# A chunked-attention and two-MLP kernel: the first blocks' values fetched by fewer loads, memory rows from GpSimd's queue

## The chip, the cores and the metric

The kernel runs on one NeuronCore of a Trainium2 chip. The time is the device time of one execution in microseconds (us). Profiles are of one execution each; the "span" is the time from its first to its last instruction. PE is TensorE, ACT ScalarE, DVE VectorE, POOL GpSimd, and SP is SyncE, which here only issues DMAs.

## The reference, cut to what matters

Attention in chunks of 32 queries: each chunk sees 8 memory rows and a window of its own keys (16 to the left, 8 to the right). Two dense layers follow, over 3072 tokens.

```python
B, H, S, D = 4, 8, 768, 64;  n_mem = 8;  chunk, left_ctx, right_ctx = (32, 16, 8)
for c in range(S // chunk):
    l_start, r_end = max(0, c_start - left_ctx), min(S, c_end + right_ctx)
    k_full = concat([mem_k, k[:, :, l_start:r_end]], axis=2)
    v_full = concat([mem_v, v[:, :, l_start:r_end]], axis=2)
    a = softmax(scale * q_c @ k_full.T)
    out[:, :, c_start:c_end] = a @ v_full
x = out.transpose(0, 2, 1, 3).reshape(B * S, H * D)          # 3072 x 512
h = x @ w_in;   g = h * clip(h + 3, 0, 6) / 6;  x = g @ w_out     # 512 -> 2048 -> 512
h = x @ w_in2;  g = where(h >= 1, h, where(h <= -1, 0, (h + 1)**2 / 4));  y = g @ w_out
```

## The kernel before, in words

**Work and tiles.** The tokens are cut into 6 tiles of 512. A tile needs the attention of four "superblocks" `s` of 128 queries (four chunks each), 24 in all. A superblock is: `scores` (L460, PE, into `sc`), a maximum over keys (L474, DVE), exponentials (L485, ACT), normalisation (L491 to L495, DVE), a transpose (L504, DVE, into `tr`), `values` (L529 in the first two tiles, PE, into `pv`), and a split of the result into a high and a low part, `xhi` (L575, ACT) and `xlo` (L579, DVE). Then the first layer runs per tile: 16 steps of `hidden` (L603 to L605, 12 matmuls into `ph`) and `project` (L652 to L654, 12 matmuls into `py`), and after six tiles the second layer does the same on `ymid`.

**Loads.** Queries and keys of a block `j` of 96 queries come in one load of 128 partitions (`load_block`, tile `q_sb`, 448 KB). Blocks below `NEARLY` lie in an array `qkv` whose rows also hold the values (512 numbers, 2048 B of a row); later ones lie in `qk` and `vv`, where a value row is cut into two of 1024 B. A superblock's values (`load_values`, tile `v_sb`, 512 KB) are, per chunk, 64 rows: 8 of the memory and 56 of the window. In the first two tiles a chunk's 64 rows stand as two columns on 32 partitions, so `load_values` cuts each chunk into pieces at rows 8, 32 and 64 and joins neighbours that continue each other; a superblock takes 7 to 9 loads of 8, 24, 32, 64 or 96 rows. The 32 weight pieces of the first layer come as 64-bit numbers (`raw`, 512 KB each, L279) and are decoded on ACT and DVE (L286 to L312) into `w`.

**Order.** A planner (`Plan.run`, L136 on) simulates the engines with a cost for every task and writes each engine's instructions in one fixed order; buffers are handed out by it too. A load is a task of SP with a cost of 430 ns, and `kb` of data that take their turn on one shared bandwidth. Every load waits for the one that stands eight places ahead of it on SP's queue, since eight completion semaphores are shared in turn. Where the planner sees PE idle in the first 60 us of its own time, matmuls on a constant tile (`warm`, L765, "fillers" below) are put in.

Of the kernel before, what the change touches and what calls it, by code (L numbers as in the profile page):

```python
# [22 lines left out]
NMEM = 8  # L23
CHUNK, LEFT, RIGHT = 32, 16, 8
# [7 lines left out]
NC = DM // 128  # L32
NF = DFF // 128
GRP = 4
NEARLY = 6
LATE_W = GRP * (QB + KB)
T = 512
NT = NTOK // T
# [38 lines left out]
class Plan:  # L77
# [58 lines left out]
    def run(self, at):  # L136
        free = dict(at)
        bw = 0
        last_kind = None
        ready = {e: [] for e in free}  # L140

        def put(t):
            for e, _ in t.ways:
                ready[e].append(t)

        for t in self.tasks:
            if not t.left:
                put(t)
        left = len(self.tasks)
        order = []  # L150
        while left:
            best = None
            for e, ts in ready.items():
                found = []
                blocked = set()
                for t in sorted(ts, key=lambda t: (t.key, t.n)) if e == "SP" else ts:
                    est = max(free[e], t.ready)
                    taken = [] if blocked & {p for b in t.bufs if not b.slot for p in b.pools} else self.slots_for(t)
                    if taken is None or len(taken) < sum(b.slot is None for b in t.bufs):
                        if e == "SP":  # L160

                            blocked.update(p for b in t.bufs if b.slot is None for p in b.pools)
                        continue
                    found.append((max([est, *(s.at + HOP for s in taken)]), t))
                if not found:
                    continue
                first = min(x[0] for x in found)
                if e == "PE" and last_kind:

                    same = [x for x in found if x[1].kind and x[0] <= free[e] + WINDOW]  # L170
                    found = same or found
                est, t = min(
                    (x for x in found if x[0] <= first + WINDOW), key=lambda x: (x[1].key, x[1].n)
                )
                if best is None or est < best[0]:
                    best = est, e, t
            assert best, ("no task can start", [
                (t.n, t.emit.__qualname__, t.key, [b.name for b in t.bufs if b.slot is None])
                for ts in ready.values() for t in ts][:20])
            est, e, t = best  # L180
            for x, _ in t.ways:
                ready[x].remove(t)
            ns = dict(t.ways)[e]
            if e == "PE":
                ns += CHANGE * (bool(t.kind) != bool(last_kind))
                last_kind = t.kind
            t.eng, t.start = e, est
            free[e] = est + ns
            t.end = est + ns + TAIL[e]
            if t.kb:  # L190
                bw = max(bw, t.end + 1900) + t.kb / 0.39
                t.end = bw
            for b, s in zip([b for b in t.bufs if b.slot is None], self.slots_for(t)):
                b.slot, s.used = s, True
            for b in t.bufs:
                b.users -= 1
                b.free_at = max(b.free_at, t.end)
                if not b.users:
                    b.slot.used, b.slot.at = False, b.free_at
            for d in t.then:  # L200
                d.left -= 1
                d.ready = max(d.ready, est)
                if not d.left:
                    put(d)
            for d in t.next:
                d.left -= 1

                alone = all(x == e for x, _ in d.ways)
                d.ready = max(d.ready, est + ns if alone else t.end + HOP)
                if not d.left:  # L210
                    put(d)
            order.append(t)
            left -= 1
        order.sort(key=lambda t: (t.start, t.n))
        return order
# [11 lines left out]
def fused_kernel(ctx: ExitStack, tc: tile.TileContext, qkv, qk, vv, wpk, const, out):  # L227
# [40 lines left out]
    def weight(l, f, z, key, after=()):  # L268
# [43 lines left out]
            eng.tensor_tensor(out=t[:, 1], in0=words()[2], in1=t[:, 0], op=ALU.subtract)  # L312

        lo, hi = (raw, "lo"), (raw, "hi")
        add(("SP", 430), key - 4, load, writes=[lo, hi], kb=512, after=after)
        add([("DVE", dve(512, True)), ("ACT", 575)], key - 0.5, shift, writes=[lo])
        add(("ACT", 575), key - 0.5, rebase, writes=[hi])
        add(("DVE", dve(512)), key - 0.4, sign, [hi], [lo])
# [21 lines left out]
    def wide(j):  # L340
        return j * NCH >= 2 * T // CHUNK

    def load_block(j, key):

        early = key < 0

        over = key > 1.75 * NF
        far = 3 * (not early)  # L350
        w = KB + KC if wide(j) else KB
        q = q_buf[j] = Buf(
            ["in"] + ["w"] * ((early or over) and not wide(j)), [128, NP * (QB + w)], F32, "q_sb",
            **({"w": 1} if early else {}),
        )
        if j < NEARLY:
            src = qkv[j, :, :WQ]
        else:
            src = qk[2 * (j - NEARLY):2 * (j - NEARLY) + 2].rearrange("g d w -> (g d) w")
        after = last_w if over else ()  # L360
        if not wide(j):
            add(("SP", 430), key - 6 - far, lambda e: nc.sync.dma_start(tile_of(q), src), writes=[(q, 0)], kb=448, after=after, line="load")
            return
        k4 = lambda: tile_of(q)[:, NP * QB:].rearrange("p (a t) -> p a t", a=NP)
        add(
            ("SP", 430), key - 6 - far, lambda e: nc.sync.dma_start(
                k4()[:, :, :KB], src[:, NP * QB:].rearrange("p (a t) -> p a t", a=NP)
            ), writes=[(q, 1)], kb=256, after=after, line="load",
        )
        add(  # L370
            ("SP", 430), key - 6 - far, lambda e: nc.sync.dma_start(tile_of(q)[:, :NP * QB], src[:, :NP * QB]),
            writes=[(q, 0)], kb=192, after=after, line="load",
        )

        def spread(e):
            k = k4()
            cast(e, k[:, :, KB + NMEM:], k[:, :, NMEM + CHUNK:KC + CHUNK])
            cast(
                e, k[:, :, 2 * CHUNK:2 * CHUNK + 2 * KC].rearrange("p a (b t) -> p a b t", b=2)[:, :, :, :NMEM],
                k[:, :, :NMEM].unsqueeze(2).to_broadcast([128, NP, 2, NMEM]),  # L380
            )

        add([("DVE", 330), ("ACT", 400)], key - 4.5, spread, [], [(q, 1)])

    def load_values(s, key):
# [4 lines left out]
        v = v_buf[s] = Buf(  # L390
            ["lv"] + ["w"] * early, [128, 2, H * D], F32, "v_sb", **({"w": 1} if early else {}),
        )
        runs = []
        for c in range(NSB):
            j, i = divmod(s * NSB + c, NCH)
            cuts = [0] + [NMEM] * (i > 0) + [CHUNK] * (not late) + [KC]
            for a, b in zip(cuts, cuts[1:]):
                row = a if b <= NMEM else a + CHUNK * i
                p, col = (64 * (c % 2) + a, c // 2) if late else (CHUNK * c + a % CHUNK, a // CHUNK)
                for r in runs:  # L400
                    if r[0] == j and r[1] + r[4] == row and r[2] + r[4] == p and r[3] == col:
                        r[4] += b - a
                        break
                else:
                    runs.append([j, row, p, col, b - a])
        for n, (j, row, p, col, m) in enumerate(sorted(runs, key=lambda r: (r[3], r[2]))):
            if j < NEARLY:
                src, rows = qkv[j, row:row + m, WQ:], lambda t: t
            else:
                g = 2 * (j - NEARLY)  # L410
                src, rows = vv[g:g + 2, row:row + m, :].rearrange("g k c -> k g c"), lambda t: t.rearrange("k (g c) -> k g c", g=2)
            add(
                ("SP", 430), key - 5 - 3 * (not early),
                lambda e, src=src, rows=rows, p=p, m=m, col=col: nc.sync.dma_start(rows(tile_of(v)[p:p + m, col]), src),
                writes=[(v, n)], kb=2 * m, line="load v",
            )
        v.parts = len(runs)

    def block(s, key):
        first = key < 0  # L420
# [89 lines left out]
        def values(e, m=None):  # L510
# [23 lines left out]

        qs = sorted({j for j, _ in places})
        add(
            ("PE", 750 if all(wide(j) for j in qs) else 1450), key - 4, scores,
            [(q_buf[j], x) for j in qs for x in range(1 + wide(j))],
            [(sc[0], 0), (sc[1], 0)], hold=[st], line="scores", kind="a",
        )  # L540
# [6 lines left out]
            add(("ACT", 1150), key - 3, lambda e, h=h: exps(e, h), [(sc[h], 0), (sm, 2)], [(st, h), (sm, 0, h)])  # L547
        add(("DVE", 280), key - 2.5, weigh, [(sm, 0, 0), (sm, 0, 1)], [(sm, 3)])
        add(("DVE", dve(512)), key - 2.4, norm, [(sm, 3)], [(st, 0), (st, 1)])
        of_v = [(v, n) for n in range(v.parts)]  # L550
        if late:
            for c in chunks:
                for b in range(2):
                    add(("DVE", dve(256)), key - 2.2, lambda e, c=c, b=b: turn_part(e, c, b), [(st, 0), (st, 1)], [(tr, c, b)])
            ts = [(tr, c, b) for c in chunks for b in range(2)]
            add(("PE", 750), key - 1, values, [*ts, *of_v], [(x, 0) for x in pv], line="values", kind="a")
        else:
            add(("DVE", 635), key - 2.2, turn, [(st, 0), (st, 1)], [(tr, 0)])
            for m in range(2):
# [128 lines left out]
    def second_x(n):  # L688
        xhi, xlo = xbuf[NT + n]
        key = NK + NF * n  # L690
        for c in range(NC):
            x = Buf(["in", "o", "st"], [128, T], F32, "x2raw")
            add(
                ("SP", 430), key - 8 + 0.5 * c, lambda e, c=c, x=x: nc.sync.dma_start(tile_of(x), ymid[n, :, c]),
                [("ymid", n, c)], [(x, 0)], kb=256, after=[h_tasks[key - NF]],
            )
            ways = [("ACT", act(T)), ("DVE", dve(T, True))]
# [138 lines left out]
```

## Time and profile before

| | |
|---|---|
| median of 3 runs | 1162.54 us (1161.67 to 1164.28) |
| the profiled execution's own time | 1161.94 us |
| its span | 1160.1 us |
| PE busy in the span | 1144.1 us (99%) |
| DVE, ACT, POOL busy | 614.9, 457.8, 0.2 us |
| granted TensorE clock, mean | 0.986 |

The profiled execution lasted 1.84 us longer than its span. A sum made on the span is brought to a time by adding that; the profiled execution is 0.6 us under the median of the three runs. PE's busy time counts fillers as work, so a busy PE is not a PE that does the reference's work.

### The profile page before, as it was taken

How to read it: one execution, taken by the hardware profiler on the slowest of the kernel's cores; microseconds unless marked ns; L12 is line 12 of the kernel's file. 1: busy time of each engine (PE TensorE's matmuls, PEld its weight loads, DVE VectorE, ACT ScalarE, POOL GpSimd, SP SyncE). 2: the span in 40 equal slices, each digit the busy share in tenths (PEclk: the TensorE clock that was granted, in tenths of full speed). 3: DMA queues.
4: the chain of work that ended last, by engine and by line, in shares of the span. 5: the costliest groups of instructions: out<-in, count | busy, mean ns of one | idle time of the engine just before them, and what ended most of it. 6: DMA issues, size and time to landing. Idle time of an engine off the chain costs nothing.

```text
span 1160.1 us, 20860 instructions
## 1 busy us (share of the span) xinstructions
PE 1144.1 (99%) x8766; PEld 939.5 (81%) x8766; DVE 614.9 (53%) x1116; ACT 457.8 (39%) x1083; POOL 0.2 (0%) x4
## 2 busy tenths in 40 slices
PE   8899999999999999999999999999999999999998
PEld 6687888888887888888888888888888888888887
DVE  2589955445555445643899634434434434433433
ACT  3599633334333333333788423223223223222221
POOL 0000000000000000000000000000000000000000
PEclk8699999999999999999999999999999999999999
DMA  6791131112112112210656300200200200000100
GB/s 207 249 396 55 57 100 35 51 54 90 48 35 87 51 51 74 70 38 19 200 183 216 91 1 1 73 1 1 73 1 1 73 1 1 37 1 1 37 1 37
DMA packets 48644, 81.05 MB, mean 70 GB/s; under 512 B 5158, under 2 KB 28582, under 8 KB 48550
## 3 DMA queue, kind: packets, MB, share of 16 engines
q1 hardware_dynamic: 48550, 79.71, 20.9%
q8 instruction: 69, 1.13, 0.4%
q14 instruction: 25, 0.20, 0.1%
HBM read 67.11 MB, written 12.58 MB: 69 GB/s over the span
## 4 chain that ended last, share of the span: by engine, by line
PE 97%; DMA 1%; issue 1%; ACT 1%; DVE 0%; SPq 0%; DVEq 0%; ACTq 0%
PE ph L603 15%; PE ph L604 15%; PE ph L605 15%; PE py L652 8%; PE po L657 8%; PE po L659 8%; PE po L658 8%; PE py L653 7%; PE py L654 7%; PE sc L460 2%; PE pv L529 2%; PE pv L519 1%; PE pv L765 1%; DMA ymid<-ysb 0%; DMA v_sb<-qkv 0%
## 5 line engine op out<-in xcount | busy, mean ns | idle before, releaser
L603 PE MATMUL ph<-xhi,w 128*128 128x512 f32 x768 | 300.5, 391 | 0.0
L604 PE MATMUL ph<-xlo,w 128*128 128x512 f32 x768 | 299.2, 390 | 0.0
L605 PE MATMUL ph<-xhi,w 128*128 128x512 f32 x768 | 299.0, 389 | 0.0
L626 ACT ACTIVATE r<-r,bias 128x512 f32<-128x512 f32 x96 | 69.3, 722 | 286.6 <-DVE r L623 286.6
L633 DVE TENSOR_TENSOR glo<-r,ghi 128x512 fp32r<-128x512 f32 x192 | 132.6, 690 | 81.9 <-ACT ghi L632 80.4
L632 ACT CAST ghi<-r 128x512 fp32r<-128x512 f32 x192 | 119.5, 623 | 133.7 <-DVE r L629 71.2
L603 PEld LDWEIGHTS ph<-xhi,w 128*128 128x128 f32 x768 | 144.5, 188 | 30.5 <-ACT raw L286 0.3
L605 PEld LDWEIGHTS ph<-xhi,w 128*128 128x128 f32 x768 | 144.3, 188 | 30.2
L604 PEld LDWEIGHTS ph<-xlo,w 128*128 128x128 f32 x768 | 144.5, 188 | 29.7
L652 PE MATMUL py<-ghi,w 128*128 128x512 f32 x384 | 153.5, 400 | 1.3 <-DVE ysb L679 1.3
L654 PE MATMUL py<-ghi,w 128*128 128x512 f32 x384 | 149.8, 390 | 0.0
L653 PE MATMUL py<-glo,w 128*128 128x512 f32 x384 | 149.8, 390 | 0.0
L657 PE MATMUL po<-w,ghi 128*128 128x512 f32 x384 | 149.4, 389 | 0.0
L658 PE MATMUL po<-w,ghi 128*128 128x512 f32 x384 | 149.4, 389 | 0.0
L659 PE MATMUL po<-w,glo 128*128 128x512 f32 x384 | 149.4, 389 | 0.0
L619 DVE SCALAR_TENSOR_TENSOR r<-r,ph 128x512 f32<-128x512 f32 x96 | 65.8, 685 | 154.0 <-ACT r L616 153.3
L623 DVE TENSOR_SCALAR r<-ph 128x512 f32<-128x512 f32 x96 | 66.3, 691 | 152.2 <-PE ph L605 152.2
L616 ACT ACTIVATE r<-ph,bias 128x512 f32<-128x512 f32 x96 | 66.2, 689 | 191.9 <-PE ph L605 191.9
L629 DVE TENSOR_TENSOR r<-ph,r 128x512 f32<-128x512 f32 x96 | 66.3, 690 | 74.7 <-ACT r L626 74.7
L652 PEld LDWEIGHTS py<-ghi,w 128*128 128x128 f32 x384 | 72.0, 188 | 18.4 <-DVE ysb L679 1.7
L654 PEld LDWEIGHTS py<-ghi,w 128*128 128x128 f32 x384 | 72.1, 188 | 15.2
L659 PEld LDWEIGHTS po<-w,glo 128*128 128x128 f32 x384 | 72.1, 188 | 15.0
(52 smaller groups left out, 962.7 us busy)
## 6 DMA issues: line engine op xcount, KB each, us to landing
raw<-wpk SPq DMA_DIRECT2D x64, 512.0 KB
ymid<-ysb SPq DMA_DIRECT2D x24, 256.0 KB
x2raw<-ymid SPq DMA_DIRECT2D x24, 256.0 KB
out<-osb SPq DMA_DIRECT2D x24, 256.0 KB
q_sb<-qk SPq DMA_DIRECT2D x21, 256.0 KB
v_sb<-vv SPq DMA_DIRECT2D x43, 112.0 KB
q_sb<-qk SPq DMA_DIRECT2D x21, 192.0 KB
v_sb<-vv SPq DMA_DIRECT2D x24, 128.0 KB
```

The costliest lines, as they stand in the source:

```text
L603: P.matmul(p, whi[:, c, :], xh[:, c, :], start=(c == 0), stop=False)
L604: P.matmul(p, whi[:, c, :], xl[:, c, :], start=False, stop=False)
L605: P.matmul(p, wlo[:, c, :], xh[:, c, :], start=False, stop=(c == NC - 1))
L626: add(("ACT", act(T) + 100), k + 0.35, lambda e: A.activation(out=rt(), in_=rt(), func=AF.Square, bias=bias[:, 1:2], scale=0.5,), [], [(r, ...
L632: add(("ACT", act(T)), k + 0.5, lambda e: A.copy(tile_of(ghi), rt()), [(r, 0)], [(ghi, 0)])
L633: add(("DVE", dve(T)), k + 0.6, lambda e: V.tensor_tensor(out=tile_of(glo), in0=rt(), in1=tile_of(ghi), op=ALU.subtract,), [(r, 0), (ghi, ...
L652: P.matmul(y, w2hi, gh, start=first, stop=False)
L653: P.matmul(y, w2hi, gl, start=False, stop=False)
L654: P.matmul(y, w2lo, gh, start=False, stop=last)
L657: P.matmul(y, gh[:, t], wt[:, 0], start=first, stop=False)
L658: P.matmul(y, gh[:, t], wt[:, 1], start=False, stop=False)
L659: P.matmul(y, gl[:, t], wt[:, 0], start=False, stop=last)
```

## The change

`load_values` of the first two tiles (superblocks 0 to 7) no longer cuts a chunk at rows 8 and 32. One load on SP's queue takes all chunks of a superblock that lie in the same block `j`: its source pattern has a step of 32 rows between the two columns, so each partition gets rows `r` and `r + 32`. For every chunk but a block's first, this puts 8 window rows where the memory's rows belong; a second load of 8 rows (16 KB), issued from GpSimd's queue, then writes the memory rows over them. It waits for the first load. There are 21 such loads. `NEARLY` becomes 11, so that all blocks of the first two tiles lie in `qkv`. The planner's numbers change too: SP's cost of a load from 430 to 450, 470 or 800 ns, the bandwidth model for loads that are not on SP, and the costs of `scores`, of late `values` and of `turn_part`.

```diff
-NEARLY = 6
+NEARLY = 11
...
             if t.kb:
                 bw = max(bw, t.end + 1900) + t.kb / 0.39
-                t.end = bw
+                t.end = bw if e == "SP" else t.end + 1900 + t.kb / 0.1
...
+        if not late:
+            v.parts = []
+            c = 0
+            while c < NSB:
+                j, i = divmod(s * NSB + c, NCH)
+                n = min(NSB - c, NCH - i)
+                rows = qkv[j, CHUNK * i:CHUNK * (i + n), WQ:]
+                src = bass.AP(rows.tensor, rows.offset, [rows.ap[0], [CHUNK * rows.ap[0][0], 2], rows.ap[1]])
+                part = (v, c)
+                v.parts.append(part)
+                add(
+                    ("SP", 470), key - 5, lambda e, src=src, p=CHUNK * c, n=n: nc.sync.dma_start(
+                        tile_of(v)[p:p + CHUNK * n], src
+                    ), writes=[part], kb=128 * n, line="load v",
+                )
+                for x in range(c + (i == 0), c + n):
+                    v.parts.append((v, "m", x))
+                    add(
+                        ("POOL", 1000), key - 4.5, lambda e, j=j, p=CHUNK * x: nc.gpsimd.dma_start(
+                            tile_of(v)[p:p + NMEM, 0], qkv[j, :NMEM, WQ:]
+                        ), [part], [(v, "m", x)], kb=16, line="load m",
+                    )
+                c += n
+            return
...
-            cuts = [0] + [NMEM] * (i > 0) + [CHUNK] * (not late) + [KC]
+            cuts = [0] + [NMEM] * (i > 0) + [KC]
...
-                ("SP", 430), key - 5 - 3 * (not early),
+                ("SP", 800), key - 8,
...
-            ("PE", 750 if all(wide(j) for j in qs) else 1450), key - 4, scores,
+            ("PE", 800 if all(wide(j) for j in qs) else 1450), key - 4, scores,
...
-                    add(("DVE", dve(256)), key - 2.2, ...
+                    add(("DVE", 450), key - 2.2, ...
-            add(("PE", 750), key - 1, values, ...
+            add(("PE", 1070), key - 1, values, ...
```

On SP, the program begins before the change with two blocks' queries and keys and then the first superblock's values in eight pieces:

```order
L362 DMA q_sb<-qkv 128x896 x2
L414 DMA v_sb<-qkv 32x512
L414 DMA v_sb<-qkv 8x512
L414 DMA v_sb<-qkv 24x512
L414 DMA v_sb<-qkv 8x512
L414 DMA v_sb<-qkv 24x512
L414 DMA v_sb<-qkv 32x512
L414 DMA v_sb<-qkv 96x512
L414 DMA v_sb<-qkv 32x512
L362 DMA q_sb<-qkv 128x896
```

After the change the same queue begins with all of the first tile's loads and goes on to the weights (`raw`), with only single loads of later blocks between them:

```order
L363 DMA q_sb<-qkv 128x896 x2
L407 DMA v_sb<-qkv 96x2x512
L407 DMA v_sb<-qkv 32x2x512
L363 DMA q_sb<-qkv 128x896
L407 DMA v_sb<-qkv 64x2x512 x2
L363 DMA q_sb<-qkv 128x896
L407 DMA v_sb<-qkv 32x2x512
L407 DMA v_sb<-qkv 96x2x512
L363 DMA q_sb<-qkv 128x896 x2
L407 DMA v_sb<-qkv 96x2x512
L407 DMA v_sb<-qkv 32x2x512
L280 DMA raw<-wpk 128x512 x2
```

Behind these rows follow one `q_sb`, six `raw`, one `q_sb`, six `raw`, and then the fifth superblock's values, the first load of values that needs a buffer which an earlier superblock held. The third `q_sb` moved from the eleventh place to the fifth, and the first `raw` from the 39th to the 15th.

GpSimd's queue held no DMA; between its constants and its end it now has the 21 loads of memory rows, 2, 3, 3 and 2 of them for the first four superblocks:

```order
L853 MEMSET const-float32-1.0 128x1
L853 MEMSET const-bfloat16-1.0 128x1
L853 MEMSET const-uint8-127 128x1
L859 UNCONDITIONAL_BRANCH
L414 DMA v_sb<-qkv 8x512 x21
L859 UNCONDITIONAL_BRANCH
```

On PE, before the change, 50 fillers stand behind the second superblock's scores, then the first superblock's values (`pv`), then the third's scores:

```order
L765 LDWEIGHTS warm
L765 MATMUL pv<-warm 128x128
L529 MATMUL pv<-tr,v_sb 64x32 x64
L460 MATMUL sc<-q_sb 32x8 x6
L460 MATMUL sc<-q_sb 32x56 x2
L460 MATMUL sc<-q_sb 32x64 x2
```

After it, the third's scores stand ahead of the first's values, with 9 fillers before and 17 behind them, and the fourth's scores follow the values:

```order
L792 LDWEIGHTS warm
L792 MATMUL pv<-warm 128x128
L556 MATMUL pv<-tr,v_sb 64x32 x64
L487 MATMUL sc<-q_sb 32x8 x4
L487 MATMUL sc<-q_sb 32x64 x2
L487 MATMUL sc<-q_sb 32x56 x4
```

Both programs run the same scores and values ahead of the first `hidden` matmul: scores of superblocks 0 to 4, values of 0 to 3. The fillers ahead of it are 26, 15, 50, 11, 6, 42, 5, 42 and 8 before (205), and 26, 9, 9, 17, 31, 2, 7 and 8 after (109). A filler is two instructions, a weight load and a matmul. Behind the first `hidden` matmuls stand 17 fillers before, and 22 and 2 after. Further on, up to the ninth superblock's scores, PE's rows differ in the places where scores and values stand between the layer's matmuls; behind those the pattern is the same in both.

## Rows read from the trace of the kernel before

**Rows 1.** The page: engines, and the instruction DMA queue (packets, MB, share).

```profile
PE 1144.1 (99%) x8766; PEld 939.5 (81%) x8766; DVE 614.9 (53%) x1116; ACT 457.8 (39%) x1083; POOL 0.2 (0%) x4
...
q8 instruction: 69, 1.13, 0.4%
```

**Rows 2.** Stretches: us; busy (instructions) of PE, PEld, DVE, ACT, POOL; clock, DMA, GB/s.

```profile
0.00:54.40 54.40, 43.57 (x1245) 35.99 (x1246) 21.80 (x63) 22.54 (x97) 0.20 (x4) 0.74 0.69 224
...
61.50:130.00 68.50, 68.47 (x855) 55.29 (x847) 64.58 (x124) 61.27 (x153) 0.00 (x0) 1.00 0.50 185
```

**Rows 3.** What PE waited for in 0:60: total us, times, longest us.

```profile
PE pv L529 <- issue: 4.5, 2, 2.9
PE sc L460 <- issue: 4.1, 4, 1.9
...
PE sc L460 <- DMA q_sb<-qkv: 0.8, 1, 0.8
```

**Rows 4.** Engines by stretch, cut where PE's idle times ended.

```profile
0.00:6.67 6.67, 5.69 (x95) 4.16 (x97) 0.13 (x3) 1.49 (x2) 0.20 (x4) 1.00 0.66 212
6.67:11.19 4.52, 3.39 (x151) 2.72 (x138) 1.07 (x5) 2.47 (x16) 0.00 (x0) 1.00 0.59 170
11.19:19.13 7.94, 6.04 (x255) 5.63 (x254) 4.91 (x14) 3.55 (x21) 0.00 (x0) 0.99 0.49 144
19.13:24.66 5.53, 3.95 (x127) 3.48 (x126) 0.93 (x3) 0.00 (x0) 0.00 (x0) 0.50 0.91 275
24.66:30.50 5.84, 4.43 (x127) 3.47 (x127) 0.97 (x4) 4.45 (x22) 0.00 (x0) 0.50 0.85 291
30.50:39.55 9.05, 8.54 (x254) 7.80 (x255) 5.54 (x15) 3.24 (x21) 0.00 (x0) 0.69 0.66 216
39.55:47.52 7.97, 5.02 (x127) 4.67 (x128) 3.98 (x8) 2.86 (x7) 0.00 (x0) 0.71 0.99 360
47.52:52.23 4.71, 4.34 (x127) 3.27 (x126) 2.09 (x6) 2.32 (x7) 0.00 (x0) 0.50 0.41 125
...
52.23:61.18 8.95, 8.94 (x127) 6.19 (x129) 8.05 (x16) 8.28 (x28) 0.00 (x0) 0.76 0.81 282
```

**Rows 5.** DMA queues in 39.6:45.1, 45.1:45.2, 47.5:49.5, 49.5:49.7, 61.2:65.1, 65.1:65.3: packets, MB, share.

```profile
q1 hardware_dynamic: 526, 1.85, 97.4%
...
q8 instruction: 1, 0.02, 61.4%
...
q1 hardware_dynamic: 278, 0.42, 68.0%
...
q8 instruction: 1, 0.02, 35.0%
...
q1 hardware_dynamic: 447, 1.63, 102.5%
...
q8 instruction: 1, 0.02, 33.6%
```

**Rows 6.** The chain that ended last, 0:56: start us, us, what.

```profile
5.95 3.91 DMA q_sb<-qkv
...
50.90 0.96 PE ph L765 x2
...
52.24 2.74 PE ph L765 x6
54.98 0.43 PE ph L603
```

**Rows 7.** SP's first issues of values in order of time: start us, us.

```profile
1.65 4.13 SPq L414 DMA_DIRECT2D v_sb<-qkv  x8
```

**Rows 8.** Fillers after the first `hidden`, and a stretch with all engines of DMA busy.

```profile
58.39 2.03 PE L765 MATMUL sc<-warm 128*128 128x256 bf16 x17
...
60.35:65.00 4.65, 4.65 (x128) 3.98 (x128) 4.62 (x10) 2.72 (x6) 0.00 (x0) 1.00 1.03 416
```

**Rows 9.** PE's groups in 0:54.42: busy us, mean ns, idle before.

```profile
L529 PE MATMUL pv<-tr,v_sb 32*64 32x32 f32 x512 | 11.9, 255 | 4.5 <-issue 4.5
```

More of the change, by code (lines that the diff above doesn't have):

```diff
@@ L314, in weight @@
         lo, hi = (raw, "lo"), (raw, "hi")
-        add(("SP", 430), key - 4, load, writes=[lo, hi], kb=512, after=after)
+        add(("SP", 450), key - 4, load, writes=[lo, hi], kb=512, after=after)
         add([("DVE", dve(512, True)), ("ACT", 575)], key - 0.5, shift, writes=[lo])
@@ L361, in load_block @@
         if not wide(j):
-            add(("SP", 430), key - 6 - far, lambda e: nc.sync.dma_start(tile_of(q), src), writes=[(q, 0)], kb=448, after=after, line="load")
+            add(("SP", 450), key - 6 - far, lambda e: nc.sync.dma_start(tile_of(q), src), writes=[(q, 0)], kb=448, after=after, line="load")
             return
@@ L365, in load_block @@
         add(
-            ("SP", 430), key - 6 - far, lambda e: nc.sync.dma_start(
+            ("SP", 450), key - 6 - far, lambda e: nc.sync.dma_start(
                 k4()[:, :, :KB], src[:, NP * QB:].rearrange("p (a t) -> p a t", a=NP)
@@ L370, in load_block @@
         add(
-            ("SP", 430), key - 6 - far, lambda e: nc.sync.dma_start(tile_of(q)[:, :NP * QB], src[:, :NP * QB]),
+            ("SP", 450), key - 6 - far, lambda e: nc.sync.dma_start(tile_of(q)[:, :NP * QB], src[:, :NP * QB]),
             writes=[(q, 0)], kb=192, after=after, line="load",
@@ L395, in load_values @@
             j, i = divmod(s * NSB + c, NCH)
-            cuts = [0] + [NMEM] * (i > 0) + [CHUNK] * (not late) + [KC]
+            cuts = [0] + [NMEM] * (i > 0) + [KC]
             for a, b in zip(cuts, cuts[1:]):
                 row = a if b <= NMEM else a + CHUNK * i
-                p, col = (64 * (c % 2) + a, c // 2) if late else (CHUNK * c + a % CHUNK, a // CHUNK)
+                p, col = 64 * (c % 2) + a, c // 2
                 for r in runs:
@@ L416, in load_values @@
             )
-        v.parts = len(runs)
+        v.parts = [(v, n) for n in range(len(runs))]
     def block(s, key):
@@ L549, in block @@
         add(("DVE", dve(512)), key - 2.4, norm, [(sm, 3)], [(st, 0), (st, 1)])
-        of_v = [(v, n) for n in range(v.parts)]
+        of_v = v.parts
         if late:
@@ L553, in block @@
                 for b in range(2):
-                    add(("DVE", dve(256)), key - 2.2, lambda e, c=c, b=b: turn_part(e, c, b), [(st, 0), (st, 1)], [(tr, c, b)])
+                    add(("DVE", 450), key - 2.2, lambda e, c=c, b=b: turn_part(e, c, b), [(st, 0), (st, 1)], [(tr, c, b)])
             ts = [(tr, c, b) for c in chunks for b in range(2)]
-            add(("PE", 750), key - 1, values, [*ts, *of_v], [(x, 0) for x in pv], line="values", kind="a")
+            add(("PE", 1070), key - 1, values, [*ts, *of_v], [(x, 0) for x in pv], line="values", kind="a")
         else:
@@ L693, in second_x @@
             add(
-                ("SP", 430), key - 8 + 0.5 * c, lambda e, c=c, x=x: nc.sync.dma_start(tile_of(x), ymid[n, :, c]),
+                ("SP", 450), key - 8 + 0.5 * c, lambda e, c=c, x=x: nc.sync.dma_start(tile_of(x), ymid[n, :, c]),
                 [("ymid", n, c)], [(x, 0)], kb=256, after=[h_tasks[key - NF]],
```

## The prediction

> **What bounds the kernel now.** The page comes first: PE is busy 99% of the span [rows 1], so time can only be won or lost where PE does something other than the reference's matmuls. The stretches show where that is [rows 2]. From 61.5 to 130 us PE is busy 68.47 of 68.50 us at the full clock, and the pattern goes on to the end. Up to 54.4 us it is busy 43.57 us, at a mean granted clock of 0.74, and 205 of its matmuls there are fillers. Everything this change touches lies in that start. So the question is when the first `hidden` matmul can run (54.98 us in the chain [rows 6]), and what follows moves with it.
>
> The view of waits says what PE stood still for in the start, and the answer is unusual: 4.5 us before `pv` and 4.1 us before `sc` with the releaser "issue" [rows 3], that is, for nothing that a semaphore tells. Cutting the start at the ends of those idle times gives the key table [rows 4]. Between them PE ran 127+126, 127+127, 127+128 and 127+126 matmuls and weight loads, and 255+254 and 254+255 where no stop shows at an edge between: always about 254, or twice that. The first row is cut where this count leads back to, at 95+97 = 192, and the last where it leads on to, 61.18 us (127+129). The page has a DMA queue of instructions with 69 packets and 1.13 MB, 16.4 KB each; 8766+8766 instructions over 69 packets is 254 per packet [rows 1]. So a packet is a block of PE's program, and PE's idle times end at block edges: it waits for its own instructions.
>
> The DMA queues show how late a block comes [rows 5]. PE enters a block at 39.55 us, and in 39.6 to 45.1 us only data moves, at a share of 97.4%; the instruction packet starts after 45.1, and PE goes on at 47.52: 5.5 us to the start and 2.4 us more. With the engines less loaded (68.0%) the block entered at 47.52 starts to load after 49.5, 2.0 us. With all of them busy on balanced transfers (102.5%), the block entered at 61.18 starts to load after 65.1, 3.9 us. The length of a block follows the DMA share in the same table [rows 4]: 4.71 us at 0.41, 3.97 at 0.49 (half of 7.94), 4.52 at 0.59 and at 0.66 (half of 9.05), 5.84 at 0.85, 5.53 at 0.91, 7.97 at 0.99. The matmuls themselves need less: all values of four superblocks are 512 in 11.9 us [rows 9], 128 of them 3.0 us.
>
> The Trainium skill, page "Runtime: NRT & Kernel Launch", section "Instruction fetch mechanics", says that the next block of 256 instructions is fetched while the current one runs, and that this is hidden. The trace agrees on the block's size, and differs on the rest: nothing else ended those 8.6 us.
>
> **The change part by part.**
>
> *Fewer loads on SP.* Before, SP spent 1.65 to 5.78 us issuing eight pieces of the first superblock's values [rows 7], and the third `q_sb` was issued at 5.95 and landed 3.91 us later [rows 6]. Now it stands fifth on SP, two issues of 4.13 / 8 us after 1.65, at about 2.7 us, and all 14 loads of the first tile (6 x 448 KB and 4 x 512 KB, 4.85 MB) go out as fast as the rule of eight lets them. Data for scores and values therefore comes earlier; at 416 GB/s [rows 8] 4.85 MB take 11.7 us. That would be a gain where PE waits for data; in the start PE's matmuls waited for a load once, 0.8 us [rows 3]. Gain on the path by itself: about 0.
>
> *What SP does instead.* It has no small pieces between, so the weights follow at once: up to the first load that waits for an older superblock's buffer there are 14 `raw` and two `q_sb`, 8.3 MB more, 13.1 MB in all, 31.5 us at 416 GB/s. Behind it come 18 more `raw`, each 1.26 us. Before, 54.4 us moved 224 GB/s x 54.4 = 12.2 MB at a share of 0.69 [rows 2]. So from about 3 us to 50 us the DMA engines now have all the work they can hold, with transfers of 400 to 500 KB eight deep, which is the state of 60 to 65 us [rows 8], and the instruction packets have to go through it.
>
> *Fewer instructions.* 205 fillers become 109 ahead of the first `hidden`: 192 instructions less, 2491 [rows 2] less 192 = 2299. Block edges lie at 192 + 256 n, so the last one ahead of it is at 2240, the eighth after 6.67 us, where before it was the ninth, at 52.23. This is the gain: one block.
>
> *The sum.* Let c be the length of a block. The first edge at 6.67 us stays (the first two `q_sb` are where they were). Then 8c, then the rest of the last values (from 2240 to 2283, 22 pairs of 11.9 / 512 us [rows 9], 0.5 us), then 8 fillers at the lower of the clock's two levels, 1.2 GHz (granted 0.50 from 47.52 to 52.23 [rows 4]), 8 x 0.43 = 3.4 us (the first `hidden` matmul of the same shape took 0.43 there [rows 6]), during which the last `xhi` and `xlo` finish. First `hidden` = 10.6 + 8c. Behind it 22 + 2 fillers stand for 17: 22 x 0.12 + 2 x 0.215 - 2.03 = +1.0 us (0.12 from 2.03 / 17 [rows 8], 0.215 as half of the 0.43 above at the full clock). Check on before: nine blocks from 6.67 to 52.23 are 5.06 us each.
>
> c with a full DMA: the nearest rows are the balanced transfers at 61.2 us, 3.9 + 2.4 = 6.3 us, and 7.97 us at a share of 0.99. PE's sequencer runs ahead of what the trace shows as executed, so it can have asked up to 0.8 us before 61.2 (the scores it was in began behind the fillers, at 58.39 + 2.03 [rows 8]), 7.1 us. I take 6.8. The first block meets a queue that is still filling: 5.5. The eighth is asked for at about 53 us, when SP waits for buffers that the third and fourth superblock hold, and a light queue gives 4.7. So 6.67 + 5.5 + 6 x 6.8 + 4.7 = 57.7, + 3.9 = 61.6, + 1.0 = 62.6 us, against 54.98: +7.6 us.
>
> *Memory rows from GpSimd.* No row shows a DMA of that queue. Below: nothing, hidden. Above: 3.91 us from issue to use, as for `q_sb` [rows 6], all ten of the first four superblocks one after the other, from about 6 us: 45 us. The fourth superblock's values are due at about 53 us in the sum above, the first's (two loads, 14 us) at about 21. I take 0; without that cover it costs from 4.7 us per load on.
>
> The Trainium skill, "DMA: Bandwidth & Descriptors", section "Anatomy of one DMA — SWDGE (gpsimd) path", gives some 2.0 us fixed for such a DMA; ten in a row would be an estimated 20 us, and the sum would stay. No run here shows it.
>
> *Decoding and the rest.* From 61.5 to 130 us DVE is busy 64.58 of 68.50 us [rows 2], so it has nearly no slack, but the decoded weights ahead of the first `hidden` are as many as before (one), and what is behind it is the same work. I take 0, and up to +4 us (the whole slack) as an unknown. Blocks 6 to 10 in long rows change packets of 1024 B to 2048 B in loads that PE does not wait for: 0.
>
> **The rivals.** The first four follow from 10.6 + 8c + 1.0 - 54.98, which is zero at c = 5.42 us.
>
> *Instruction blocks come as before or faster* (ends on the other side). For it: six of the nine blocks were under 5.42, and the two of 5.5 and 5.8 lay among loads of 8 and 24 rows, which the change removes. Against it: c rose with the DMA share, and the share rises. c = 5.06: -2.9 us, 1159.0. c = 4.2, about the mean of the lightest four: -9.8 us, 1152.1. It decides below c = 5.13.
>
> *No fetch limit at all.* If blocks cost nothing, the first `hidden` could not be earlier than PE's busy time, 43.57 us [rows 2] less 96 fillers of 0.12, 32 us, nor later than the 44.2 of c = 4.2; the middle, 38, is -16 us, 1146. The idle times at the edges speak against it. By the skill's page named above, whose section calls the fetch hidden, this is the case that holds.
>
> *It cancels*: c between 5.13 and 5.71, -2.3 to +2.3 us.
>
> *Worse than forecast.* c = 7.97, the row at 0.99, in all eight blocks: 75.4, +20.4 us, 1182.3. Against it: one row alone shows it, and the block entered at 61.18 had fuller engines and less delay.
>
> *GpSimd's rows late*, from 4.7 us per load in series; then PE waits in the values, not at block edges.
>
> **How the numbers follow.** The profiled execution took 1161.94 us; with +7.6 that is 1169.5. It stands 0.6 us under the median, well inside 0.2% (2.3 us), which is about what a measurement of this kernel can tell from no change. Chances: blocks slowed as forecast or more, 0.53; GpSimd's rows or the decoding late and slower by that, 0.05; cancelled, 0.12; blocks as before or faster, 0.25; no fetch limit, 0.05. So slower 0.58, same 0.12, faster 0.30. The likeliest's own range is 1165 (c = 5.85 throughout, +3.4) to 1182. The range over all cases leaves out about one in ten at the bottom (c near 4.2 or less) and somewhat less at the top: 1153 to 1178.
>
> **What would show it.** Right: PE's idle times with the releaser "issue" again lie 254 instructions apart, 6 to 7 us each, with instruction packets starting 3.5 us or more after an edge; the DMA share is above 0.9 from 5 to 45 us; the first `hidden` comes at 59 to 64 us; from there PE is busy without a gap. Wrong: blocks of 4 to 5 us at a full DMA share (then the share is not what delays them), a first `hidden` before 53 us, or PE waiting for `v_sb` from GpSimd.

## The result, and the profile after

The changed kernel takes 1176.87 us (median of 4 runs, 1176.21 to 1177.19) against 1162.11 us for the kernel before in the same session: a ratio of 1.0125, interval 1.0107 to 1.0143. It is slower by 14.8 us, about twice the 7.6 us forecast. The profiled execution took 1176.9 us, its span 1175.1 us.

The page of the changed kernel, the lines that answer to [rows 1]:

```profile
PE 1139.8 (97%) x8677; PEld 935.1 (80%) x8677; DVE 613.6 (52%) x1110; ACT 461.9 (39%) x1089; POOL 11.1 (1%) x25
...
q8 instruction: 68, 1.11, 0.4%
q0 software_dynamic: 672, 0.35, 0.1%
```

PE does less work in a longer span (the last line is the queue of GpSimd's loads). The view of waits of PE in 0:90 (columns as in [rows 3]) says where it stands still:

```profile
PE pv L556 <- issue: 15.1, 5, 4.1
PE sc L487 <- issue: 12.5, 3, 5.2
PE sc L487 <- DMA q_sb<-qkv: 1.3, 1, 1.3
PE sc L792 <- DVE bias L772: 1.0, 1, 1.0
PE sc L792 <- ACT st L512: 0.6, 1, 0.6
```

The idle time with the releaser "issue" went from 9.0 us (the 8.6 of [rows 3] and 0.4 in front of a filler) to 27.6 us; no other wait grew by more than 0.6 us. It stands at eight places, and cutting the start there gives the table that answers to [rows 4]:

```profile
0.00:6.45 6.45, 5.46 (x94) 4.05 (x96) 0.13 (x3) 1.49 (x2) 0.20 (x4) 1.00 0.73 224
6.45:14.23 7.78, 2.75 (x152) 2.18 (x138) 1.07 (x5) 2.47 (x16) 2.69 (x5) 0.84 1.06 269
14.23:21.80 7.57, 3.99 (x128) 2.85 (x128) 2.61 (x7) 2.47 (x16) 1.54 (x3) 0.71 1.04 284
21.80:28.93 7.13, 4.67 (x127) 4.26 (x126) 2.93 (x8) 1.93 (x11) 1.03 (x2) 0.51 1.04 374
28.93:35.58 6.65, 2.54 (x128) 2.27 (x128) 1.52 (x6) 1.63 (x10) 0.00 (x0) 0.50 1.02 405
35.58:41.92 6.34, 3.35 (x125) 3.23 (x126) 2.01 (x5) 1.99 (x12) 0.00 (x0) 0.50 1.05 364
41.92:50.23 8.31, 5.34 (x127) 4.97 (x127) 2.42 (x8) 2.45 (x12) 1.55 (x3) 0.71 1.03 271
50.23:58.62 8.39, 3.14 (x129) 2.50 (x129) 2.98 (x6) 2.76 (x6) 0.27 (x1) 0.50 1.05 265
58.62:65.05 6.43, 3.90 (x127) 3.43 (x127) 1.18 (x3) 0.98 (x3) 1.28 (x3) 0.50 1.04 379
65.05:69.64 4.59, 4.59 (x39) 2.51 (x40) 3.07 (x7) 3.50 (x8) 0.00 (x0) 0.50 1.01 400
```

Eight blocks of some 254 PE instructions, each 6.3 to 8.4 us long, with PE busy for 2.5 to 5.3 of it. The DMA share (last but one; the summed time of the packets over that of 16 engines, so it can pass 1) is above 1.0 in every row after the first, and the granted clock is at 0.50 or 0.51 in six of the ten, the lower of its two levels.

The DMA queues of the changed kernel, in 35.58:39.2, 39.2:39.4 and 41.92:47.8 (packets, MB, share; they answer to [rows 5]):

```profile
q1 hardware_dynamic: 409, 1.49, 103.0%
...
q1 hardware_dynamic: 21, 0.08, 96.4%
q8 instruction: 1, 0.02, 33.5%
...
q1 hardware_dynamic: 459, 1.28, 103.7%
```

PE enters a block at 35.58; for 3.6 us only data moves, then the instruction packet starts, and PE, which had run out of instructions at 38.93, goes on at 41.92. Over the eight blocks the packet starts 5.14, 4.60, 4.51, 3.85, 3.7, 5.94, 5.82 and 3.84 us after the edge (before: 0.7 to 5.6, mean 2.4), and PE goes on 2.4 to 3.0 us after that start.

The end of the start, in the chain that ended last (columns as in [rows 6]):

```profile
58.62 0.51 PE sc L487 x11
59.13 0.86 PE pv L792 x7
59.99 2.53 PE pv L556 x96
62.52 2.53 issue
65.05 1.07 PE pv L556 x30
66.12 3.52 PE ph L792 x8
69.64 0.35 PE ph L630
```

The first `hidden` is at 69.64 there, 54.98 before: +14.66 us. By its own record, which begins 0.56 us earlier in both, it starts at 69.08 and 54.42; from here on this second number is used (the expectations give 54.98 for before and 69 for after). Span less first `hidden` is 1160.1 - 54.42 = 1105.7 before and 1175.1 - 69.08 = 1106.0 after. So the whole loss is made ahead of that matmul.

### The profile page after: what moved, and what is told of

It is laid out like the page before. It is cut to its first block, busy times and chain, and to the rows that moved or that the text cites. A ratio compares the mean times of both kernels' runs of the same rounds, so it can differ in the third digit from the quotient of the medians.

```text
span 1175.1 us, 20688 instructions
## 1 busy us (share of the span) xinstructions
PE 1139.8 (97%) x8677; PEld 935.1 (80%) x8677; DVE 613.6 (52%) x1110; ACT 461.9 (39%) x1089; POOL 11.1 (1%) x25
## 4 chain that ended last, share of the span: by engine, by line
PE 94%; DMA 3%; issue 1%; DVE 1%; ACT 0%; SPq 0%; DVEq 0%; ACTq 0%
PE ph L630 15%; PE ph L631 15%; PE ph L632 15%; PE py L679 8%; PE po L686 7%; PE po L685 7%; PE po L684 7%; PE py L680 7%; PE py L681 7%; DMA v_sb<-qkv 2%; PE pv L556 2%; PE pv L546 1%; PE sc L487 1%; DMA raw<-wpk 1%; DMA ymid<-ysb 1%
## 5 line engine op out<-in xcount | busy, mean ns | idle before, releaser
L684 PEld LDWEIGHTS po<-w,ghi 128*128 128x128 f32 x384 | 72.2, 188 | 15.0
```

What stands on the lines that cost most here:

```text
L684: P.matmul(y, gh[:, t], wt[:, 0], start=first, stop=False)
```

## The experiments

Each was timed beside the kernel before, in four further sessions in which that kernel took 1161.2 to 1162.0 us; "first `hidden`" and "rest" (span less first `hidden`) are of its one profiled execution.

| kernel | time, us | ratio to before (interval) | first `hidden` | rest |
|---|---|---|---|---|
| before | 1162.11 | | 54.42 | 1105.7 |
| after | 1176.87 | 1.0125 (1.0107 to 1.0143) | 69.08 | 1106.0 |
| after, no memory rows | 1175.45 | 1.0116 (1.0095 to 1.0137) | 68.24 | 1104.5 |
| before, with copies | 1183.87 | 1.0189 (1.0165 to 1.0213) | 77.14 | 1106.3 |
| after, 4 weight pieces | 1163.52 | 1.0021 (1.0008 to 1.0034) | 54.35 | 1107.5 |
| after, 26 fillers | 1169.39 | 1.0064 (1.0044 to 1.0084) | 63.54 | 1106.4 |
| after, 4 pieces, 26 fillers | 1162.53 | 0.9999 (0.9982 to 1.0015) | 49.06 | 1110.1 |
| before, 26 fillers | 1153.91 | 0.9925 (0.9902 to 0.9949) | 47.47 | 1105.8 |
| after, 6 pieces behind `q_sb`, 26 fillers | 1159.52 | 0.9979 (0.9965 to 0.9992) | 49.63 | 1109.4 |
| before, 11 long blocks | 1161.59 | 0.9994 (0.9978 to 1.001) | 53.95 | 1111.4 |
| after, half depth | 1165.43 | 1.0033 (1.002 to 1.0047) | 62.20 | 1106.0 |
| after, half depth, 26 fillers | 1159.06 | 0.9978 (0.9966 to 0.9989) | 51.42 | 1107.0 |
| after, quarter depth | 1193.87 | 1.0274 (1.0253 to 1.0295) | 72.25 | 1119.2 |
| before, 6 pieces, 26 fillers | 1153.61 | 0.9926 (0.99 to 0.9953) | 45.39 | 1105.8 |

Of the long-block and half-depth kernels the profiled execution was the slowest of ten, 5.5 and 4.6 us above the median, so their times are read from the medians, and their first `hidden` and rest are those of a late execution.

**GpSimd's loads taken out.** The queue entry stays, without its load.

```diff
-                        ("POOL", 1000), key - 4.5, lambda e, j=j, p=CHUNK * x: nc.gpsimd.dma_start(
-                            tile_of(v)[p:p + NMEM, 0], qkv[j, :NMEM, WQ:]
-                        ), [part], [(v, "m", x)], kb=16, line="load m",
+                        ("POOL", 1000), key - 4.5, lambda e: None, [part], [(v, "m", x)], kb=16, line="load m",
```

> The changed kernel without its 21 loads of memory rows from GpSimd's queue (it leaves out the memory rows of all chunks but a block's first, so those chunks see window rows in their place); the order on every other engine is unchanged. Theory (PE waits for its blocks of instructions behind a full DMA queue): nothing changes, blocks of 6.3 to 8.4 us as in the changed kernel, first hidden at 68 to 71 us, 1174 to 1178 us. Rival (GpSimd's loads, late or in the way of the instruction packets): the blocks come faster or PE no longer waits, first hidden before 65 us, 1172 us or less.

Measured: 1175.45 us, the blocks 6.3 to 8.4 us long as with the loads, 26.4 us of "issue". At most 1.4 us of the loss is GpSimd's. The timeline of POOL in the changed kernel shows why: the ten loads that the first four superblocks need are issued by 23.7 us, 0.5 us each.

```profile
7.75 1.14 POOL L414 DMA_DIRECT2D v_sb<-qkv  x2 [7.30 <-DMA v_sb<-qkv]
...
22.64 1.03 POOL L414 DMA_DIRECT2D v_sb<-qkv  x2 [4.82 <-DMA v_sb<-qkv]
47.51 1.68 POOL L414 DMA_DIRECT2D v_sb<-qkv  x3 [23.84 <-PE pv L556]
```

**The kernel before with its queues filled from elsewhere.**

```diff
+        pad = [dram.tile([128, 512], I64, tag=f"pad{i}", name=f"pad{i}") for i in range(4)]
+        for i in range(24):
+            nc.gpsimd.dma_start(pad[i % 4], wpk[1, i % NF, 0])
```

> The kernel before with 24 added copies of 512 KB from HBM to an unused HBM buffer, issued from GpSimd's queue from the start, four in flight; order of all other engines unchanged. Theory: with the DMA queue filled by strangers the kernel before shows the changed kernel's blocks, 6 to 8 us each with instruction packets starting 3.5 us or more after an edge, first hidden at 63 to 78 us instead of 55, 1170 to 1185 us. Rival (the new order of the loads or of PE makes the changed kernel slow, not the load on the queue): blocks stay at 4 to 5.8 us, first hidden under 60 us, 1161 to 1167 us.

Measured: 1183.87 us, first `hidden` at 77.14. The view of waits of PE in 0:80 of this kernel:

```profile
PE sc L460 <- DMA q_sb<-qkv: 23.7, 4, 13.5
PE pv L529 <- issue: 4.7, 2, 2.4
PE sc L460 <- issue: 3.6, 1, 3.6
PE ph L768 <- issue: 3.2, 1, 3.2
```

Most of the loss is PE's wait for its queries and keys; "issue" rose only from 9.0 to 11.5 us. The copies slowed the data itself, so the time and the first `hidden`, both in the theory's ranges, are there for another reason, by luck: on what late blocks cost this run is inconclusive. The packets did start late, 5.1 and 4.1 us after the edges at 30.38 and 44.68 us.

**Few weight pieces under way.** The undecoded weights of the first layer are held to four of their buffers, so SP issues the fourth `raw` at 19.1 us and the fifth at 51.8, once the first is decoded. Up to the first `hidden`, PE runs the changed kernel's instructions one for one.

```diff
+NRAW = 4
...
-                    if len(free) > b.keep.get(p, 0):
+                    if p == "w" and b.early:
+                        if b.name == "raw":
+                            free = [s for s in free if s.n < NRAW]
+                        else:
+                            free = [s for s in free if s.n >= NRAW] or (free if b.name == "w" else [])
+                    if len(free) > (0 if b.name == "raw" and b.early else b.keep.get(p, 0)):
...
+        raw.early = w.early = l == 0
```

> The changed kernel with the first layer's undecoded weights held to four buffers of the same pool, so that only four weight pieces (2 MB) are loaded before decoding frees one; PE's order up to the first 24 hidden matmuls is unchanged. Theory: the first three edges stay (14, 22, 29 us), then the queue runs dry and the blocks take 4 to 5 us, first hidden at 52 to 58 us, and the time falls to 1158 to 1167 us. Rival (PE's new order, or its waits for values, set the start): first hidden stays at 66 us or later, 1172 us or more.

Measured: 1163.52 us, first `hidden` at 54.35: some 13 of the 14.8 us are back (13.4 between the medians, 12.9 when each is set against the kernel before of its own session). Its stretches, cut at its edges:

```profile
7.14:15.57 8.43, 2.75 (x153) 2.18 (x139) 1.07 (x5) 2.48 (x16) 2.69 (x5) 0.86 1.06 228
15.57:23.41 7.84, 3.99 (x128) 2.85 (x128) 2.61 (x7) 2.47 (x16) 1.55 (x3) 0.72 1.05 262
23.41:30.38 6.97, 4.78 (x127) 4.30 (x126) 2.93 (x8) 1.93 (x11) 1.03 (x2) 0.50 0.96 336
30.38:34.35 3.97, 2.54 (x127) 2.24 (x127) 1.53 (x6) 1.62 (x10) 0.00 (x0) 0.50 0.37 106
34.35:38.16 3.81, 3.36 (x125) 3.26 (x126) 1.31 (x4) 1.61 (x10) 1.55 (x3) 0.50 0.25 75
38.16:44.00 5.84, 5.84 (x125) 5.58 (x127) 2.04 (x7) 1.94 (x13) 1.26 (x3) 0.50 0.34 98
44.00:46.98 2.98, 2.98 (x139) 2.48 (x135) 2.55 (x7) 2.66 (x8) 0.28 (x1) 0.50 0.07 17
```

One program shows both conditions. While the first tile's loads and four weights are under way the blocks take 7.0 to 8.4 us; then the queues go quiet, the packets start 0.7 to 1.4 us after an edge, and the same matmuls, at the same lower clock, take 3.0 to 4.0 us, or 5.84 with PE busy throughout. The later weights cost little: the rest is 1.4 us longer than with the change. This is the run that shows the cause: what the change loses is time for instruction blocks, and how long the later ones take is set by the weights that SP now issues early. The first three it leaves as long as they were, 23.2 us (7.14 to 30.38) where the kernel before took 12.5 us for three (6.67 to 19.13 in [rows 4]). There the first tile's own loads, now issued at once, fill the queues: in the changed kernel the first late packet starts at 11.59 us, and the first weight is not issued before 11.82. So the 13 us come back in the later blocks, and the cost of the first three stays.

**Fewer fillers.** Only the 26 in front of the first scores are kept.

```diff
-FILL = 60000
+FILL = 6000
```

> The changed kernel without fillers but for the first 26, so 83 matmuls (166 instructions) fewer ahead of the first hidden one and 24 fewer behind it. Theory: one block edge less to wait for and no 8 fillers in front of the first hidden one, so it comes 8 to 12 us earlier, at 58 to 62 us, and the time is 1165 to 1170 us although the clock is lower. Rival (the wait is for data or for ACT and DVE, fillers only fill it): first hidden stays within 2 us of 69.6, 1174 to 1179 us.

Measured: 1169.39 us, 7.5 us less than the change, first `hidden` at 63.54: one block fewer. The blocks that are left are as long (6.2 to 9.3 us): fillers between the blocks cost as instructions to be fetched. The eight in front of the first `hidden`, 3.52 us in the chain above, went too, so not all of the gain is fetching.

The same line in the kernel before, and with four weight pieces in the changed kernel:

> The kernel before with only the first 26 fillers kept, 179 fillers (358 instructions) less, which is one to two blocks. Theory: blocks of 4 to 6 us as before, less some 6 to 8 us and the fillers ahead of the first hidden matmul: it comes at 46 to 51 us instead of 54.98, 1155 to 1159 us. Rival (the fillers cost nothing, since values and scores wait for data, DVE or ACT underneath them): first hidden at 53 to 55 us, PE's idle time moves from issue to those releasers, 1161 to 1164 us.

> The change, with at most four weight pieces of the first layer on their way at once in the start, and only the first 26 fillers kept. Theory (PE's blocks of 256 instructions are late when the DMA queues are full of data): the first three blocks as slow as in the kernel with few weight pieces (8.4, 7.9, 7.0 us), the later ones near 4 us or under, and, with 166 instructions less, one block fewer, so the first hidden matmul at 47 to 50 us instead of 54.4 and a time of 1156 to 1160 us. Rival (without fillers PE's slower level, or the chain over DVE and ACT, takes over what the blocks gave back): first hidden at 53 to 56 us, PE's idle time with releasers on DVE or ACT instead of issue, a time of 1162 to 1166 us.

Before without those fillers: 1153.91 us, first `hidden` at 47.47. It is 8.1 us faster than the kernel before (1162.04 us beside it), a little more than the theory's amount; up to 3.7 us of it can be the eight fillers that stood right in front of the first `hidden` (two pieces of [rows 6]). Its view of waits in 0:70 shows that what lies under the blocks is now as large as the blocks:

```profile
PE sc L460 <- DMA q_sb<-qkv: 5.4, 2, 5.0
PE pv L529 <- issue: 5.0, 4, 2.3
PE pv L529 <- DVE tr L504: 4.8, 2, 2.6
PE sc L460 <- issue: 3.1, 1, 3.1
```

The changed kernel with four pieces and 26 fillers met its forecast for the first `hidden` (49.06) and missed the one for the time, 1162.53 instead of 1156 to 1160: the rest grew to 1110.1. Its waits in 49:140:

```profile
PE ph L638 <- DVE r L654: 2.4, 2, 1.4
PE sc L495 <- issue: 1.9, 1, 1.9
PE py L688 <- DVE glo L668: 0.9, 1, 0.9
```

In 60:70 DVE is busy 9.97 of 10.00 us there. That the late weights push their decoding on DVE into that stretch is the likely reason; it was not separated.

**Weights behind the queries.** As in the four-piece kernel with 26 fillers, with six pieces, and the first tile's `q_sb` on the same six buffers:

```diff
-NRAW = 4
+NRAW = 6
...
-                        if b.name == "raw":
+                        if b.name in ("raw", "q_sb"):
```

> The change, with only the first 26 fillers kept, six weight pieces on their way at once in the start, and the first tile's queries and keys sharing the weights' buffers, so that from the third piece on a weight waits for PE's scores. Theory: the queues run dry earlier, so the third block is lighter already: blocks of 7 to 8, 5 to 7, then 4 to 5 us, first hidden at 44 to 48 us, 1152 to 1158 us. Rival (the weights then come too late, and PE waits for the first decoded weight or runs out of weights behind the first hidden matmul): PE's idle time behind that matmul rises from 1.3 us to 5 us or more, and the time is 1160 us or more.

Measured: 1159.52 us, first `hidden` at 49.63, blocks of 8.3, 8.8, 6.6, 5.1, 4.1, 4.5 and 3.4 us. The first three are all above what the theory has, and so is the first `hidden`. Behind it PE idles 4.5 us up to 140 us, close to the rival's 5. The time lies between the two.

**Long rows alone.** `NEARLY = 11` in the kernel before, nothing else.

> The kernel before with the first eleven blocks in long rows, and nothing else of the change: PE, DVE and ACT run the same instructions in the same order, SP one load less. Theory: no change, 1160 to 1164 us, first hidden at 53 to 57 us, since packets of 2048 bytes in place of 1024 change neither the bytes nor the depth of the queues in the first 30 us. Rival (the long rows themselves crowd out the instruction packets): blocks of 6 us or more from the fourth on, 1166 us or more.

Measured: 1161.59 us, ratio 0.9994, as the theory has it. This part of the change is neutral.

**Half and quarter depth.** Each load on SP waits for the one eight places ahead. A tiny load behind each large one halves the large ones under way; three quarter them, for SP's first 30 loads. PE's instructions and their order stay.

```diff
+SMALL = 30
...
+    small = [dram.tile([1, 64], F32, name=f"small{i}") for i in range(8)]
...
             t.emit(t.eng)
+            if t.eng == "SP" and t.kb and loads_seen < SMALL:
+                nc.sync.dma_start(small[loads_seen % 8], qkv[0, :1, :64])
+                loads_seen += 1
```

> The change, with one load of 256 bytes behind each of SP's first 30 loads. Since each load waits for the one eight places ahead of it, at most four large transfers instead of eight are then under way. Bytes, loads, PE's instructions and their order stay. Theory (an instruction packet waits behind the data queued ahead of it, so its delay goes with the depth of the queues): fetch delays fall from 4 to 6 us to 2 to 3.5 us in the first eight blocks, these become 4.5 to 6 us long, first hidden at 50 to 59 us instead of 69, and a time of 1157 to 1166 us. Rival (the delay goes with the share of the engines' time that data takes, whatever the depth): while the share stays above 0.9 the delays stay at 4 to 6 us, first hidden at 65 us or later, 1172 us or more.

> The same with only the first 26 fillers kept, which is 166 instructions less. Theory: two to three blocks of 4.5 to 6 us fewer than that many full ones ask for, first hidden at 44 to 52 us, 1151 to 1159 us; set against the kernel before without those fillers (1153.9 us) it shows whether fewer loads for the values are worth anything once the queues are shallow. Rival (depth does not matter): first hidden at 60 us or later, 1167 us or more, as with the fillers left out alone (1169.4 us).

> The change with three loads of 256 bytes behind each of SP's first 30 loads, so that at most two large transfers are under way; SP then issues four loads for one large, some 2 us for 512 KB, so the share of the engines' time falls too. Theory: fetch delays of 1 to 2 us, blocks of 3.5 to 5 us as in the kernel before, and data that comes later instead; first hidden at 46 to 58 us, PE's idle time with releaser issue under 10 us in all, 1155 to 1166 us. Rival (depth does not matter, or data that comes later costs more than the blocks give back): first hidden at 62 us or later, 1168 us or more.

Half depth: 1165.43 us, inside the theory's range and 11.4 us less than the change. The first `hidden`, at 62.20, lies between the two; this execution stood 4.6 us above the median, and with the same rest the median puts it at some 57.6 us (an estimate), inside the theory's range. The packets start 0.8, 2.0, 4.6, 3.5, 4.0, 2.9, 3.9 and 5.3 us after an edge, mean 3.4 where the change has 4.7. The two shortest delays lie where the share was 0.96 and 0.90 instead of 1.05 and 1.04, and the last tiny load is issued at 44.65 us, so the block entered at 50.24, with the 5.3 us, is not one at half depth. The fair comparison is 20:40, with a share of 1.02 against 1.03: delays of 3.5, 4.0 and 2.9 us against 4.5, 3.9 and 3.7. So depth matters at the same share, but less than in proportion, and how much of the 11.4 us is depth and how much a lower share at the start stays open. With 26 fillers: 1159.06 us, the theory's upper end, first `hidden` at 51.42. Set against the 1153.91 us of the kernel before with 26 fillers, no gain from fewer loads for the values shows here either.

Quarter depth missed the theory's time and its first `hidden`, and met the rival's: 1193.87 us and 72.25. Its waits in 0:95, and its queues in 33.78:39.3:

```profile
PE sc L490 <- DMA q_sb<-qkv: 17.3, 5, 7.0
PE pv L559 <- issue: 9.3, 5, 2.9
PE sc L490 <- issue: 5.5, 1, 5.5
```

```profile
q1 hardware_dynamic: 468, 0.79, 70.5%
q0 software_dynamic: 64, 0.03, 2.4%
```

The data is late, as the rival says; and the packets still start 2.8 to 5.6 us after an edge, at a share of 0.70 and with 0.79 MB moved in 5.5 us. In 10:70 the engines moved 127 GB/s, against 301 with half depth, so the tiny loads cost bandwidth as well, and this run does not test depth alone.

**Fewer weight pieces in the kernel before.** The edit of the four-piece kernel with `NRAW = 6` and `FILL = 6000`, in the kernel before.

> The kernel before with only the first 26 fillers kept and at most six weight pieces on their way at once in the start, where ten were issued by 42 us in the kernel before without fillers. Theory: the blocks entered from 27 to 45 us, 6 us long there, come down to 4 to 5 us, so the first hidden matmul comes at 42 to 46 us instead of 47.5; the weights behind it come later, which cost 2 to 4 us in the kernels with few pieces, so the time is 1149 to 1155 us against 1153.9. Rival (what holds the first hidden matmul there is data for scores or the work of DVE and ACT, not blocks): first hidden at 47 to 49 us and a time of 1155 to 1159 us, the later weights being all that changes.

Measured: 1153.61 us, first `hidden` at 45.39, 2.1 us earlier than with fewer fillers alone, and a rest no longer. Both are where the theory has them, but the time cannot be told from 1153.91. The two beat the kernel before by some 0.75% and are the fastest versions found.

## Why the prediction was right, and what was mis-sized

**Right:** the bound (PE's instruction blocks), the sign, the place (eight blocks, and nothing lost behind the first `hidden`), and the zeros: GpSimd's rows (1175.45 us without them), the long rows (ratio 0.9994), the data that comes earlier (PE still waits for one load, 1.3 us), decoding (rest +0.3 us). GpSimd's zero held by its cover: the loads took a median of 5.9 us to land, more than the 3.91 us of the prediction's upper price, but the ten were issued by 23.7 us, before the first values ran at 24.0. The prediction's test for "right" asked for idle times 254 instructions apart, packets 3.5 us or more after an edge and a share above 0.9 from 5 to 45 us; all three hold. Its 6 to 7 us each (2.5 to 5.3 for the idle times, 6.3 to 8.4 for the blocks) and its first `hidden` at 59 to 64 us do not, and behind that matmul stands one gap, of 0.6 us. The time lies only 1.1 us under the upper end of the range.

The rival that no fetch limit exists, which the Trainium skill, page "Runtime: NRT & Kernel Launch", section "Instruction fetch mechanics", would make the case ("mostly hidden"), falls: taking away early weights, without touching PE's instructions, gave some 13 us back.

**Mis-sized:** the term c, the length of a block. Against the sum's 61.57 us to the first `hidden` (69.64 measured, by the chain):

| term | forecast | measured | off by |
|---|---|---|---|
| first edge | 6.67 | 6.45 | -0.22 |
| first block | 5.5 | 7.78 | +2.28 |
| six blocks | 40.8 | 44.39 | +3.59 |
| eighth block | 4.7 | 6.43 | +1.73 |
| end and 8 fillers | 3.9 | 4.59 | +0.69 |

Behind the first `hidden`, where +1.0 was forecast, the rest grew by 0.3. Beside the six in the middle, two steps failed. "The first block meets a queue that is still filling": it was full, at a share of 1.06 from 6.45 us on. "The eighth is asked for at about 53 us, when SP waits for buffers": it was asked for at 58.62, after SP had issued the sixth superblock's values at 46.12 and gone on to 13 more weights, from 48.15 to 66.6, so there was no light end. SP's timeline:

```profile
46.12 1.17 SPq L407 DMA_DIRECT2D v_sb<-qkv  x2
48.15 18.46 SPq L280 DMA_DIRECT2D raw<-wpk  x13
```

Most of the table's last row is a count: the prediction takes 256 instructions to a block where the trace records some 254, so the last edge stood at 2223 and not at 2240, and 30 matmuls of the last values were left (1.07 us) instead of 22 (0.5).

For the six in the middle, 6.8 came, in the main, from a stretch with `raw` alone (61.2 to 65.1 us before). The four blocks of the changed kernel in which mostly weights and queries move (21.80 to 41.92, and the eighth) took 6.3 to 7.1 us, as forecast, at 364 to 405 GB/s. The four in which values are loaded took 7.6 to 8.4 us: at the same share the queues moved 265 to 284 GB/s. In all eight blocks 1.3 to 1.7 MB of data moved between the edge and the packet's start. So the better term is this amount over the rate of the queues at that moment: 1.49 MB at some 410 GB/s are 3.6 us, 1.28 MB at some 220 GB/s are 5.9 us. The amount is no more than delay times rate; what is found is that it varies less than the delays, which go from 3.7 to 5.9 us. That the packet waits behind a given amount of queued data is how these numbers are read, and not shown; in the kernel before the amount was 0.42 and 1.85 MB in two stretches of [rows 5], with half depth it was 0.2 to 1.5 MB, and at quarter depth the reading could not be tested. What sets the amount stays open.

## What to carry to other kernels

Where PE runs hundreds of short matmuls while SP floods the queues, look at PE's waits at every 256th instruction before anything else. Idle time without a releaser there was instruction fetch in this case, and it was paid once per block, so each filler or split instruction costs its share of a block. Small loads in front can be worth keeping for what they hold back (argued; no run puts them back alone): here the edit that freed SP's queue let the next transfers start, and these crowded out the instruction packets, a wait that no semaphore shows. Holding back weights that were not yet needed gave most of the loss back, and dropping most fillers from the kernel before won 0.75%.

## What the runs showed of the hardware

An instruction packet took about 1 us, and PE went on 2.4 to 3.0 us after it started, wherever it had waited for it in the changed kernel and in the one with four weight pieces; the start itself came 0.7 to 1.4 us after an edge in quiet queues and 3.7 to 5.9 us in full ones. PE had only the block it was in to run meanwhile: with 2.5 to 5.3 us of work in a block it idled 2.5 to 5.3 us at an edge. A GpSimd load of 8 rows took 0.52 us to issue, and 5.9 us (median of 21) to land.
